# Fourier, RWKV mix and Mish MLP on one core: output steps in thirds, weight sums made earlier, another layout for the last tile

## The chip, the cores and the metric

The kernel runs on one core of a Trainium2 chip, as one program with one launch. The metric is the time of one execution on the device in microseconds (us). The engines of the core run side by side and wait for each other by semaphores: TensorE (PE, with its weight loads shown as PEld), VectorE (DVE), ScalarE (ACT), GpSimd (POOL) and SyncE (SP), which issues most of the DMAs.

## The reference

Three layers run one after another over 4 sequences of 3072 tokens with 256 channels:

```
X = rfft(x, axis=1);  Y = shrink(X mixed by w_r, w_i, plus biases);  a = irfft(Y)
xk, xr = mixes of a[token] and a[token - 1]
m = sigmoid(xr @ w_r) * (relu(xk @ w_k)**2 @ w_v)              # RWKV channel mix, 256 -> 1024 -> 256
h = m @ w_in;  out = (h * tanh(softplus(h))) @ w_out             # Mish MLP, 256 -> 2048 -> 256
```

The kernel writes each operand of a large product as a high and a low part and adds three products (high by high, low by high, high by low).

## The kernel before, in words

The program has three stages. The Fourier stage (to about 276 us) and the mix (to about 936 us) prepare the input `x2d` of the MLP in DRAM. The MLP (from there to the end) takes 24 tiles of 512 tokens.

**The mix** loops over 32 tiles `t` of 384 tokens, each in four sub-steps `i2` = 0 to 3. In a sub-step TensorE computes two blocks of `kp` (`emit_k`), and then two blocks of `vp` from the squared `kp` of two sub-steps before (`emit_v`). In sub-step 1 it also computes the gate `pp` (`emit_r`). ScalarE turns `kp` into `kr` (relu), `kh` and `kr` again (squares), and VectorE makes `kl`, the low part. In sub-step 2 VectorE multiplies the finished `vp` of the tile before by its gate into `r` (`v_ev`). The `vp` of the next tile goes to the same PSUM bank, so its first weight load waits for that `r`. The MLP's weights are decoded and split into parts in the gaps of this loop: a queue `bgq` of generators is advanced by `bg(n)`, n steps in each sub-step, 4, 1, 2 and 3 of them. A step is one instruction or two on VectorE or ScalarE, or none (some only let a load come in). Each engine runs its instructions in the order in which the program emits them.

**The MLP** works on pairs of 128 hidden rows, the steps `P` = 8t + q (q = 0 to 7 within a tile). In tile 0 the first product is made in the plain way (`emit_h`). From tile 1 on it is made by Strassen and Winograd's scheme (`emit_hS`): seven products of half-blocks instead of eight, for which sums of input blocks (`make_xS`) and of weight blocks (`WS`, and one that overwrites a part of `WI`) are needed. The second product (`o_steps`) of step P - 3 is dealt out among the first product of step P: `o(n1)`, `o(n2)` and `o(99)` take as many matmuls from it at three places. Even steps from 8 on use Strassen's scheme there too (`strassen`), with 21 matmuls of 256 columns. The others take 12 matmuls of 512 columns. A step P that is odd therefore carries the 21 small matmuls of the even step P - 3, and an even step the 12 large ones. I call them odd and even steps.

The three places cover three reads of a PSUM bank `xy` that TensorE writes again afterwards:

```
prod(xy[:, 0, :], A(0, 0), 0, start=True);  copy z <- xy on ScalarE;     o(n1)
prod S_(1), S_(2), A(0, 1);                 copy ub <- xy on ScalarE;    o(n2)
prod S_(0);                                 z <- xy + ub on VectorE;     o(99)
prod S3, A(1, 1)
```

So the first weight load of `S_(1)` waits for the copy `z`, that of `S_(0)` for the copy `ub`, and that of `S3` for the addition `z`. n1 and n2 were 3 and 2 products (9 and 6 matmuls, 6 left) in odd steps, and 5 and 3 matmuls (4 left) in even ones.

The weight sums `WS` are made by `make_WS` on VectorE and ScalarE, for a quarter of the hidden rows each: three quarters in steps 2, 4 and 6 of tile 0, and the last quarter over steps 8 to 11. Results of a tile leave by `put_out`: two transposes on VectorE and 16 DMAs of 32 KB in pieces of 256 bytes. For the last tile that comes after the last matmul, with the DMAs dealt out to three queues.

Of the kernel before, what the change touches and what calls it, by code (L numbers as in the profile page):

```python
# [29 lines left out]
def kernel(  # L30
# [887 lines left out]
    for t in range(NA + 1):  # L918
# [5 lines left out]
        for i2 in range(4):  # L924
# [47 lines left out]
            bg((4, 1, 2, 3)[i2])  # L972
# [29 lines left out]
    def make_WS(q, late=False):  # L1002

        if late:
            both = w2p.tile([128, 2, 1024], F32, tag="x2h", name="was", bufs=1)
            a, sm = both[:, 0].rearrange("p (j r i n) -> p j r i n", j=2, r=2, i=2), both[:, 1]
            sm = sm.rearrange("p (r k n) -> p r k n", r=2, k=4)
        else:
            a = pb.tile([128, 2, 2, 2, 128], F32, tag="S", name="wa", bufs=1)
            sm = pb.tile([128, 2, 4, 128], F32, tag="HS", name="ws", bufs=1)  # L1010
        w = WI[:, :, :, 512 * q:512 * (q + 1)]
        fl = a.rearrange("p j r i n -> p j (r i n)")
        nc.vector.tensor_tensor(out=fl, in0=w[:, :, 0, :], in1=w[:, :, 1, :], op=ALU.add)
        yield
        for k, x0, x1, op in (
            (0, a[:, 0, :, 1, :], a[:, 1, :, 1, :], ALU.add), (1, sm[:, :, 0, :], a[:, 0, :, 0, :], ALU.subtract),
            (2, a[:, 0, :, 0, :], a[:, 0, :, 1, :], ALU.subtract), (3, a[:, 1, :, 0, :], sm[:, :, 1, :], ALU.subtract),
        ):
            nc.vector.tensor_tensor(out=sm[:, :, k, :], in0=x0, in1=x1, op=op)
        yield  # L1020
        hi, lo = (
            (
                (WS[:, 2 * q:2 * q + 2, :, l, :], sm[:, :, 0:3, :]),
                (w[:, 0, l, :].rearrange("p (r i n) -> p r i n", r=2, i=2)[:, :, 1, :], sm[:, :, 3, :]),
            ) for l in range(2)
        )
        for h, v in hi:
            nc.scalar.copy(out=h, in_=v)
        yield
        for (h, _), (l, v) in zip(hi, lo):  # L1030
            nc.vector.tensor_tensor(out=l, in0=v, in1=h, op=ALU.subtract)

    xS_t, xT_t = {}, {}

    def make_xS(t, k, eng=None):

        v = x2_t[t]
        b11, b12, b21, b22 = (v[:, j, 256 * h:256 * h + 256] for j in range(2) for h in range(2))
# [4 lines left out]
        raw = [  # L1043
            [(xS[:, l, 0, :], b11), (xS[:, l, 1:3, :], v[:, 1, :].rearrange("p (h n) -> p h n", h=2))]
            for l in range(2)
        ]

        def sub(o, x0, x1):
            nc.vector.tensor_tensor(out=xT[:, o, :], in0=x0, in1=x1, op=ALU.subtract)

        def cast(o, x):
            if eng is None:
                nc.vector.tensor_copy(out=o, in_=x)
            else:
                eng.copy(out=o, in_=x)

        if k == 0:
            sub(0, b12, b11)
            sub(2, b22, b12)
        elif k == 1:  # L1060
            sub(1, b22, xT[:, 0, :])
            sub(3, b21, xT[:, 1, :])
        elif k == 2:
            cast(xS[:, 0, 3:7, :], xT)
        elif k == 3:
            nc.vector.tensor_tensor(out=xS[:, 1, 3:7, :], in0=xT, in1=xS[:, 0, 3:7, :], op=ALU.subtract)
        elif k == 4:
            for xs, b in raw[0]:
                cast(xs, b)
        else:  # L1070
            for (xl, b), (xh, _) in zip(raw[1], raw[0]):
                nc.vector.tensor_tensor(out=xl, in0=b, in1=xh, op=ALU.subtract)
# [9 lines left out]
    def strassen(P):  # L1082
        return P >= 8 and P % 2 == 0
# [80 lines left out]
    def put_out(t, engs):  # L1164
# [6 lines left out]
        n = 0  # L1171
        for m in range(4):
# [3 lines left out]
            for i in range(4):  # L1176
                engs[n % len(engs)].dma_start(
# [3 lines left out]
                n += 1  # L1181

    def act_1(P):
        t, r = divmod(P, 8)
        if r == 2 and t > 1:
            new_U(t - 1)
            nc.scalar.copy(out=U_t[t - 1][:, 0, :], in_=o_t[t - 1][2][:, 0, :])
        mish_xy(P - 1)

    def dve_1(P):  # L1190
        t, r = divmod(P, 8)
        if r == 2 and t > 1:
            first_sums(t - 1)
        if r == 3 and t > 0:
# [10 lines left out]
        if r == 7 and t > 0:  # L1205
            put_out(t - 1, (nc.sync,))
# [13 lines left out]
    def emit_hS(P, o):  # L1220
# [16 lines left out]
        n1, n2 = (3, 2) if strassen(P - LAG) else (5, 3)  # L1237
# [23 lines left out]

    def o_steps(P):
# [27 lines left out]
        for k in (1, 6, 5, 7, 2, 4, 3) if q == 0 else (1, 2, 4, 6, 5, 7, 3):  # L1290
# [5 lines left out]
            yield  # L1296
# [37 lines left out]
    last_sums(NBLK - 1)  # L1334
    put_out(NBLK - 1, (nc.sync, nc.scalar, nc.gpsimd))
# [82 lines left out]
```

## Time and profile before

| what | value |
|---|---|
| median of 3 runs | 1947.49 us (1946.81 to 1949.35) |
| the profiled execution | 1950.29 us, of which the span shown by the profile is 1948.5 us |
| TensorE busy, weight loads busy | 1924.0 us (99%), 1812.8 us (93%) |
| VectorE, ScalarE, GpSimd busy | 1360.7 us (70%), 1291.6 us (66%), 134.2 us (7%) |
| chain that ended last | TensorE 97%, DMA 1%, ScalarE 1%, VectorE 1% |

A busy TensorE here is an engine with a matmul in its pipeline. Matmuls overlap, so the share does not tell how closely they follow each other. That is read from the start times of consecutive matmuls and weight loads. The granted clock of TensorE (PEclk) is a share of full speed, 1.00 for 2.4 GHz and 0.50 for 1.2 GHz.

### The profile page before, as it was taken

What the parts mean: (1) busy time and instruction counts of PE and PEld (TensorE: products, weight loads), DVE (VectorE), ACT (ScalarE), POOL (GpSimd) and SP (SyncE); (2) the same over time, 40 slices, a digit from 0 to 9 for tenths busy, and PEclk for the clock granted to TensorE, in tenths of its full rate; (3) what the DMA queues carried; (4) which work ended last, traced back from release to release, by engine and by line L of the source; (5) the groups of instructions that cost most, each with busy time, mean ns of one, the idle gap of its engine ahead of it and who ended that gap; (6) DMA issues with size and microseconds to landing.
All of it is one profiled execution on the core that took longest, in us unless ns stands there. A gap on an engine that the chain in (4) does not pass through costs nothing.

```text
span 1948.5 us, 32822 instructions
## 1 busy us (share of the span) xinstructions
PE 1924.0 (99%) x12718; PEld 1812.8 (93%) x12718; DVE 1360.7 (70%) x2384; ACT 1291.6 (66%) x2244; POOL 134.2 (7%) x241
## 2 busy tenths in 40 slices
PE   7999999999999999999999999999999999999998
PEld 5888889999999999999799999999999999999997
DVE  2788775655656656644587877777777778777776
ACT  3666666666666666666467777667777667777664
POOL 0444430000000000000000000000000000000000
PEclk8999999999999999999999999999999999999999
DMA  9777532112222221211100011110011110010101
GB/s 285 218 238 229 164 101 72 60 61 61 69 61 63 80 73 56 65 50 36 63 22 23 23 28 28 30 26 23 22 31 26 30 26 23 23 32 24 30 15 22
DMA packets 114912, 127.23 MB, mean 65 GB/s; under 512 B 60722, under 2 KB 90644, under 8 KB 114756
## 3 DMA queue, kind: packets, MB, share of 16 engines
q1 hardware_dynamic: 110292, 112.22, 20.2%
q0 software_dynamic: 3744, 12.75, 1.8%
q8 instruction: 100, 1.64, 0.4%
q14 instruction: 56, 0.46, 0.1%
q10 hardware_dynamic: 720, 0.16, 0.0%
HBM read 72.65 MB, written 52.43 MB: 64 GB/s over the span
## 4 chain that ended last, share of the span: by engine, by line
PE 97%; DMA 1%; ACT 1%; DVE 1%; SPq 0%; issue 0%; POOL 0%; DVEq 0%; POOLq 0%
PE o L1272 26%; PE xy L1231 21%; PE kp L718 14%; PE vp L903 14%; PE mxp L440 4%; PE pp L857 3%; PE z L1231 3%; PE pp L541 3%; PE s2p L384 2%; PE i1p L482 2%; PE s1p L335 2%; PE k1p L440 2%; DMA XS<-in_x_dram 1%; PE hp L823 1%; DMA yc<-in_w_i_dram 0%; PE h0p L823 0%
## 5 line engine op out<-in xcount | busy, mean ns | idle before, releaser
L1272 PE MATMUL o<-gh,WO 128*128 128x512 f32 (+1 forms) x1168 | 321.3, 359 | 0.0
L718 PE MATMUL kp<-xk,WK 128*128 128x384 f32 x1524 | 291.9, 339 | 0.0
L890 DVE TENSOR_TENSOR kl<-kr,kh 128x768 fp32r<-128x768 f32 x128 | 123.0, 961 | 232.1 <-ACT kr L889 232.1
L903 PE MATMUL vp<-kh,WV 128*128 128x384 f32 x1024 | 280.4, 335 | 0.0
L718 PEld LDWEIGHTS kp<-xk,WK 128*128 128x128 f32 x1524 | 264.1, 188 | 0.6 <-ACT yT L550 0.4
L1231 PE MATMUL xy<-xS,WS 128*128 128x256 f32 x1656 | 257.6, 282 | 3.6 <-ACT z L1239 3.5
L1231 PEld LDWEIGHTS xy<-xS,WS 128*128 128x128 f32 x1656 | 235.9, 190 | 20.8 <-ACT z L1239 4.2
L1231 PE MATMUL xy<-xS,WI 128*128 128x256 f32 x1656 | 237.2, 287 | 0.0
L1096 DVE TENSOR_TENSOR gl<-g,gh 128x512 fp32r<-128x512 f32 x368 | 222.7, 615 | 20.5 <-ACT g L1094 20.4
L1231 PEld LDWEIGHTS xy<-xS,WI 128*128 128x128 f32 x1656 | 212.8, 188 | 20.1 <-DVE z L1115 5.1
L1272 PEld LDWEIGHTS o<-gh,WO 128*128 128x128 f32 x1168 | 200.8, 189 | 18.4
L1272 PE MATMUL o<-gl,WO 128*128 128x512 f32 (+1 forms) x584 | 209.3, 358 | 0.0
L1094 ACT ACTIVATE gh<-z 128x512 fp32r<-128x512 f32 x184 | 110.3, 599 | 144.4 <-DVE z L1115 87.9
L903 PEld LDWEIGHTS vp<-kh,WV 128*128 128x128 f32 x1024 | 186.7, 188 | 0.2 <-DVE r L911 0.2
L1115 DVE TENSOR_TENSOR z<-xy,ub 128x256 f32<-128x256 f32 x184 | 79.4, 432 | 135.8 <-PE xy L1231 125.5
L903 PE MATMUL vp<-kl,WV 128*128 128x384 f32 x512 | 171.5, 335 | 0.0
L888 ACT ACTIVATE kh<-kr 128x768 fp32r<-128x768 f32 x128 | 108.2, 845 | 95.4 <-PE vp L903 95.2
L1245 ACT COPY ub<-xy 128x512 f32<-128x512 f32 x184 | 108.1, 588 | 89.3 <-PE xy L1231 89.3
L881 ACT ACTIVATE kr<-kp 128x768 f32<-128x768 f32 x127 | 103.4, 814 | 70.6 <-PE kp L718 68.5
L1272 PE MATMUL o<-HS,WT 128*128 128x256 f32 x828 | 128.5, 282 | 0.0
L1272 PEld LDWEIGHTS o<-gl,WO 128*128 128x128 f32 x584 | 110.5, 189 | 9.2
L1115 DVE TENSOR_TENSOR HS<-S,HS 128x1024 fp32r<-128x1024 f32 x92 | 111.8, 1216 | 0.3 <-ACT HS L1134 0.2
(176 smaller groups left out, 3555.1 us busy)
## 6 DMA issues: line engine op xcount, KB each, us to landing
scr<-Cs SPq DMA_DIRECT2D x48, 256.0 KB, 2.4
D<-scr SPq DMA_DIRECT2D x32, 384.0 KB, 3.8
x2d<-r POOLq DMA_DIRECT2D x32, 384.0 KB, 2.8
x<-x2d SPq DMA_DIRECT2D x24, 512.0 KB, 3.9
out_dram<-ob SPq DMA_DIRECT2D x374, 32.0 KB, 1.6
A<-scr SPq DMA_DIRECT2D x44, 256.0 KB, 3.7
xs<-in_x_dram SPq DMA_DIRECT2D x24, 384.0 KB, 5.6
scr<-xs SPq DMA_DIRECT2D x24, 384.0 KB, 3.9
```

The lines of the kernel that those rows point to most:

```text
L440: nc.tensor.matmul(out=out, lhsT=a, rhs=w, start=(start and i == 0), stop=(stop and i == len(ts) - 1))
L718: nc.tensor.matmul(out=p, lhsT=WK[:, dh, w, f * 128:(f + 1) * 128], rhs=hl[:, v, dh, :], start=(i == 0), stop=(i == 5),)
L881: nc.scalar.activation(out=kr, in_=kp_t.pop(P)[:, :, 0:TA], func=AF.Relu)
L888: nc.scalar.activation(out=kh, in_=kr, func=AF.Square)
L890: nc.vector.tensor_tensor(out=kl, in0=kr, in1=kh, op=ALU.subtract)
L903: nc.tensor.matmul(out=p[:, o, 0:TA], lhsT=WV[:, f, w, o * 128:(o + 1) * 128], rhs=v[:, m, :], start=(f == 0 and i == 0), stop=(f == 7 and ...
L1094: nc.scalar.activation(out=h[:, v[1], :], in_=src[:, v[0], :], func=AF.Mish)
L1096: lambda: nc.vector.tensor_tensor(out=gl[:, hs[1], :], in0=g[:, hs[1], :], in1=gh[:, hs[1], :], op=ALU.subtract)
L1115: nc.vector.tensor_tensor(out=out, in0=x0, in1=x1, op=op)
L1231: nc.tensor.matmul(out=out, lhsT=a(l), rhs=xS[:, v, b, :], start=(start and n == 0), stop=False, skip_group_check=True)
L1245: nc.scalar.copy(out=ub, in_=xy)
L1272: nc.tensor.matmul(out=out, lhsT=w, rhs=v, start=start, stop=False, skip_group_check=True)
```

## The change

It has three parts.

1. **Output steps.** In Strassen steps `o_steps` now yields after each matmul, and not after each product of three. The 21 matmuls of an odd step are dealt out as 7, 7 and 7, and the 12 of an even one as 4, 4 and 4.
2. **Weight sums.** `make_WS` is gone from the MLP. A new generator `bg_S` makes the same sums for an eighth of the hidden rows at a time within the mix, behind the weights that it needs, and stores them in DRAM (`ws_d`). The MLP loads them by 16 DMAs on SyncE's queue. `bg` now takes 2 steps in sub-step 1 (it was 1).
3. **Last tile.** Its second product has the tokens on the output's partitions (`last_steps`): the activations are the stationary operand and `WO`, high and low parts side by side, is the moving one, 8 times 512 and 256 columns in each step. It uses no Strassen scheme, so `strassen` is false for this tile. `make_xS` puts its tokens in another order, by reading floats that stand 32 apart. As each block of 128 tokens is finished, `last_out` adds the two halves (ScalarE copies one, VectorE adds the other) and stores them by one DMA of 128 KB.

```diff
+    def bg_S(pool, w, r):
+        w = w[:, :, :, 256 * r:256 * r + 256]
+        a = pool.tile([128, 2, 2, 128], F32, tag="dec_v", name="wa", bufs=1)
+        sm = pool.tile([128, 4, 128], F32, tag="dec_b", name="ws", bufs=1)
+        nc.vector.tensor_tensor(
+            out=a.rearrange("p j i n -> p j (i n)"), in0=w[:, :, 0, :], in1=w[:, :, 1, :], op=ALU.add
+        )
+        yield
+        for k, x0, x1, op in (
+            (0, a[:, 0, 1], a[:, 1, 1], ALU.add), (1, sm[:, 0], a[:, 0, 0], ALU.subtract),
+            (2, a[:, 0, 0], a[:, 0, 1], ALU.subtract), (3, a[:, 1, 0], sm[:, 1], ALU.subtract),
+        ):
+            nc.vector.tensor_tensor(out=sm[:, k, :], in0=x0, in1=x1, op=op)
+            if k % 2:
+                yield
+        hl = pool.tile([128, 4, 2, 128], F32R, tag="wt", name="wshl", bufs=1)
+        nc.scalar.copy(out=hl[:, :, 0, :], in_=sm)
+        yield
+        nc.vector.tensor_tensor(out=hl[:, :, 1, :], in0=sm, in1=hl[:, :, 0, :], op=ALU.subtract)
+        yield
+        nc.sync.dma_start(out=ws_d[r], in_=hl.rearrange("p k l d -> p (k l d)").bitcast(F32))
...
+        for r in (2 * q, 2 * q + 1):
+            bgq.append(bg_S(pap, WI, r))
...
-            bg((4, 1, 2, 3)[i2])
+            bg((4, 2, 2, 3)[i2])
...
-    def make_WS(q, late=False):
...
+    def load_WI(r):
+        nc.sync.dma_start(
+            out=WI[:, 0, :, 256 * r + 128:256 * r + 256].bitcast(F32),
+            in_=ws_d[r][:, 768:1024].rearrange("p (l n) -> p l n", l=2),
         )
...
+    def last_order(a, how="p (c w n) -> p c w n"):
+        return a.rearrange(how, n=4, w=32)
...
+        last = t == NBLK - 1
+        o4 = last_order if last else (lambda a, how=None: a)
+        b11, b12, b21, b22 = (
+            o4(v[:, j, 256 * h:256 * h + 256], "p (c n w) -> p c w n") for j in range(2) for h in range(2)
+        )
...
     def strassen(P):
-        return P >= 8 and P % 2 == 0
+        return 8 <= P < 8 * (NBLK - 1) and P % 2 == 0
...
-        n1, n2 = (3, 2) if strassen(P - LAG) else (5, 3)
+        n1, n2 = (7, 7) if strassen(P - LAG) else (3, 2) if P - LAG >= 8 * (NBLK - 1) else (4, 4)
...
+    def last_steps(q, o, gh, gl):
+        for m in (2, 3, 0, 1):
+            for m2 in range(2):
+                f = 2 * q + m2
+                ms = slice(m * 128, (m + 1) * 128)
+                nc.tensor.matmul(out=o[m], lhsT=gh[:, m2, ms], rhs=WO[:, f], start=(f == 0), stop=False)
+                nc.tensor.matmul(
+                    out=o[m][:, 0, :], lhsT=gl[:, m2, ms], rhs=WO[:, f, 0, :], start=False, stop=(f == 15)
+                )
+                if q == 7 and m2:
+                    last_out(m, o[m])
+                yield
...
+    def last_out(m, o):
...
+        nc.scalar.copy(out=v, in_=o[:, 1])
+        nc.vector.tensor_tensor(out=v, in0=v, in1=o[:, 0], op=ALU.add)
...
+        nc.sync.dma_start(out=out_v[b, j, k].rearrange("n w d -> w n d"), in_=ob)
...
                 mm(o[bank][:, half, :], w(l), rhs, q == 0 and bank not in begun)
                 begun.add(bank)
-            yield
+                yield
...
     load_x2(1)
+    for r in range(8):
+        nc.sync.dma_start(out=WS[:, r].bitcast(F32).rearrange("p k l d -> p (k l d)"), in_=ws_d[r][:, 0:768])
+    for r in range(2):
+        load_WI(r)
     for i in range(4):
         nc.sync.dma_start(out=WT[:, i].bitcast(F32).rearrange("p k l d -> p (k l d)"), in_=wt_d[i])
...
-                if P == 8:
-                    last_WS = make_WS(3, True)
                 emit_hS(P, o)
-                if P < 12:
-                    next(last_WS, None)
...
-                if q in (2, 4, 6):
-                    for _ in make_WS(q // 2 - 1):
-                        pass
+                load_WI(P)
...
-    last_sums(NBLK - 1)
-    put_out(NBLK - 1, (nc.sync, nc.scalar, nc.gpsimd))
```

On TensorE an odd step stood like this before, from the last three of its first nine output matmuls on (`o<-...` are output matmuls; `xy<-xS,WS x6` are `S_(1)` and `S_(2)`, `xy<-xS,WS x3` is `S_(0)`, and `xy<-xS,WI x9` begins with `S3` and ends with the next step's first product):

```order
L1272 MATMUL o_9562<-gh,WT 128x256 x2
L1272 MATMUL o_9562<-gl,WT 128x256
L1231 MATMUL xy<-xS,WS 128x256 x6
L1231 MATMUL z<-xS,WI 128x256 x3
L1272 MATMUL o_9564<-HS,WT 128x256 x3
L1272 MATMUL o_9565<-HS,WT 128x256 x3
L1231 MATMUL xy<-xS,WS 128x256 x3
L1272 MATMUL o_9565<-HS,WT 128x256 x3
L1272 MATMUL o_9563<-HS,WO 128x256 x3
L1231 MATMUL xy<-xS,WI 128x256 x9
```

The same odd step on TensorE now, from the seventh and last of its first output matmuls on:

```order
L1312 MATMUL o_9633<-gh,WT 128x256
L1241 MATMUL xy<-xS,WS 128x256 x6
L1241 MATMUL z<-xS,WI 128x256 x3
L1312 MATMUL o_9633<-gh,WT 128x256
L1312 MATMUL o_9633<-gl,WT 128x256
L1312 MATMUL o_9635<-HS,WT 128x256 x3
L1312 MATMUL o_9636<-HS,WT 128x256 x2
L1241 MATMUL xy<-xS,WS 128x256 x3
L1312 MATMUL o_9636<-HS,WT 128x256 x4
L1312 MATMUL o_9634<-HS,WO 128x256 x3
L1241 MATMUL xy<-xS,WI 128x256 x9
```

Two matmuls left the first group, and one was added to each of the other two, so seven stand ahead of `S3` where six stood.

ScalarE in sub-steps 0 and 1 of the mix's tile 7 before (`yT` is the next tile's input, `r<-pp` the gate at the start of sub-step 2):

```order
L550 COPY yT<-pp 128x3x128
L881 ACTIVATE kr<-kp 128x768
L888 ACTIVATE kh<-kr 128x768
L889 ACTIVATE kr<-kr 128x768
L550 COPY yT<-pp 128x3x128
L881 ACTIVATE kr<-kp 128x768
L888 ACTIVATE kh<-kr 128x768
L889 ACTIVATE kr<-kr 128x768
L866 ACTIVATE r<-pp 128x768
```

ScalarE at the same place now:

```order
L574 COPY yT<-pp 128x3x128
L165 CAST wshl<-ws 128x4x128
L907 ACTIVATE kr<-kp 128x768
L914 ACTIVATE kh<-kr 128x768
L915 ACTIVATE kr<-kr 128x768
L574 COPY yT<-pp 128x3x128
L165 CAST wshl<-ws 128x4x128
L907 ACTIVATE kr<-kp 128x768
L914 ACTIVATE kh<-kr 128x768
L915 ACTIVATE kr<-kr 128x768
L892 ACTIVATE r<-pp 128x768
```

In each of these two sub-steps a cast of weight sums now stands ahead of the relu `kr<-kp`. VectorE in sub-step 1 of the same tile now, from the `kl` of sub-step 0 on:

```order
L916 TENSOR_TENSOR kl<-kr,kh 128x768
L585 TENSOR_TENSOR dl<-yT 128x768
L161 TENSOR_TENSOR ws<-wa 128x128
L161 TENSOR_TENSOR ws<-wa,ws 128x128
L916 TENSOR_TENSOR kl<-kr,kh 128x768
L937 TENSOR_TENSOR r<-r,vp 128x768
```

Two subtractions of `bg_S` stand between `dl` and `kl` (one decoding instruction stood there before), and ScalarE's second cast reads what they write.

## Rows read from the trace of the kernel before

**Rows 1.** Windows: us, busy of PE, PEld, DVE, ACT, POOL, PEclk, DMA, GB/s.

```profile
276.00:930.00 654.00, 654.00 (x3932) 652.87 (x3931) 377.21 (x529) 437.74 (x628) 23.90 (x32) 1.00 0.21 62
...
967.00:971.00 4.00, 0.51 (x3) 0.11 (x1) 2.47 (x6) 3.37 (x7) 0.00 (x0) 0.98 0.30 117
971.00:974.30 3.30, 3.30 (x13) 3.02 (x14) 0.82 (x1) 0.59 (x1) 0.00 (x0) 0.51 0.00 0
...
1014.00:1900.00 886.00, 885.97 (x6373) 830.32 (x6372) 698.23 (x1398) 621.66 (x1189) 0.00 (x0) 1.00 0.11 26
```

**Rows 2.** Chain of waits in one odd and one even step: start, us, what.

```profile
1387.12 0.71 PE o L1272 x6
1387.84 1.22 PE xy L1231 x9
...
1392.33 0.93 PE o L1272 x4
1393.26 1.07 PE xy L1231 x9
```

**Rows 3.** Timeline of the next odd step, around S3: start, us, what.

```profile
1397.66 0.43 DVE L1115 TENSOR_TENSOR z<-xy,ub 128x256 f32<-128x256 f32 x1 [0.94 <-PE xy L1231]
1397.75 0.52 PE L1272 MATMUL o<-HS,WO 128*128 128x256 f32 x3
...
1398.15 0.55 PEld L1231 LDWEIGHTS xy<-xS,WI 128*128 128x128 f32 x4
```

**Rows 4.** Timeline, copy z and the load of S_(1): even step, then odd.

```profile
1389.15 0.36 ACT L1239 COPY z<-xy 128x256 f32<-128x256 f32 x1 [0.37 <-PE xy L1231]
...
1389.82 0.90 PEld L1231 LDWEIGHTS xy<-xS,WS 128*128 128x128 f32 x6
...
1394.43 0.36 ACT L1239 COPY z<-xy 128x256 f32<-128x256 f32 x1 [0.27 <-PE xy L1231]
...
1395.13 0.55 PEld L1231 LDWEIGHTS xy<-xS,WS 128*128 128x128 f32 x4
```

**Rows 5.** Waits of the weight loads, 970 to 1940 us: total, times, longest.

```profile
PEld xy L1231 <- DVE z L1115: 5.1, 23, 0.5
PEld xy L1231 <- ACT z L1239: 4.2, 2, 3.9
```

**Rows 6.** Timeline of ScalarE at step 8, start of tile 1.

```profile
967.47 0.83 ACT L1028 CAST WS<-ws 128x768 fp32r<-128x768 f32 x1 [5.16 <-DVE ws L1019]
```

**Rows 7.** Timeline of the mix, tile 10, sub-steps 1 and 2.

```profile
502.93 0.95 DVE L561 TENSOR_TENSOR dl<-yT 128x768 f32<-128x768 f32 x1
...
505.37 0.85 ACT L888 ACTIVATE kh<-kr 128x768 fp32r<-128x768 f32 x1 [1.32 <-PE vp L903]
...
507.13 0.96 DVE L890 TENSOR_TENSOR kl<-kr,kh 128x768 fp32r<-128x768 f32 x1 [3.25 <-ACT kr L889]
...
508.00 0.95 DVE L911 TENSOR_TENSOR r<-r,vp 128x768 f32<-128x768 f32 x1
...
509.11 0.19 PEld L903 LDWEIGHTS vp<-kh,WV 128*128 128x128 f32 x1
```

**Rows 8.** Groups by form: count, busy us, mean ns of one, idle before.

```profile
L881 ACT ACTIVATE kr<-kp 128x768 f32<-128x768 f32 x127 | 103.4, 814 | 70.6 <-PE kp L718 68.5
...
L141 ACT CAST wthl<-wt 128x512 fp32r<-128x512 f32 x4 | 2.5, 620 | 6.2 <-DVE wt L132 6.2
...
L132 DVE TENSOR_TENSOR wt<-dec_v,wt 128x128 f32<-128x128 f32 x8 | 2.3, 290 | 0.1
```

**Rows 9.** The end: last matmul; DMA rate, 1939.4 to 1948.5 in 40 slices.

```profile
1939.01 0.40 PE L1272 MATMUL o<-gl,WO 128*128 128x512 f32 x1
...
GB/s 0 0 0 0 0 0 0 0 0 0 0 0 109 161 107 183 134 221 231 122 228 183 177 180 168 105 0 0 0 0 0 0 0 0 0 0 0 0 0 0
```

**Rows 10.** The page's DMA issues: KB each, median us from issue to landing.

```profile
scr<-Cs SPq DMA_DIRECT2D x48, 256.0 KB, 2.4
...
out_dram<-ob SPq DMA_DIRECT2D x374, 32.0 KB, 1.6
```

More of the change, by code (lines that the diff above doesn't have):

```diff
@@ L64 @@
     wt_d = [dram.tile([128, 1024], F32, name=f"wt_{i}") for i in range(4)]
+    ws_d = [dram.tile([128, 1024], F32, name=f"ws_{r}") for r in range(8)]
     x2d = [dram.tile([128, 2, 1536], F32, name=f"x2d_{q}") for q in range(2 * B)]
@@ L1000 @@
     WT = pb.tile([128, 4, 4, 2, 128], F32R, name="WT")
-    def make_WS(q, late=False):
[L1004 to L1013, printed above, removed]
-        yield
[L1015 to L1025, printed above, removed]
-        )
[L1027 to L1031, printed above, removed]
+    def load_WI(r):
+        nc.sync.dma_start(
+            out=WI[:, 0, :, 256 * r + 128:256 * r + 256].bitcast(F32),
+            in_=ws_d[r][:, 768:1024].rearrange("p (l n) -> p l n", l=2),
+        )
     xS_t, xT_t = {}, {}
+    def last_order(a, how="p (c w n) -> p c w n"):
+        return a.rearrange(how, n=4, w=32)
     def make_xS(t, k, eng=None):
         v = x2_t[t]
-        b11, b12, b21, b22 = (v[:, j, 256 * h:256 * h + 256] for j in range(2) for h in range(2))
+        last = t == NBLK - 1
[3 more added lines that the diff above has]
+        )
         if k == 0:
@@ L1042, in make_xS, with raw, xt @@
         xT, xS = xT_t[0], xS_t[t]
[L1043 to L1046, printed above, removed]
+        def raw(l):
+            if last:
+                return [(o4(xS[:, l, i, :]), b) for i, b in enumerate((b11, b21, b22))]
+            return [(xS[:, l, 0, :], b11), (xS[:, l, 1:3, :], v[:, 1, :].rearrange("p (h n) -> p h n", h=2))]
+        def xt(o):
+            return o4(xT[:, o, :])
         def sub(o, x0, x1):
-            nc.vector.tensor_tensor(out=xT[:, o, :], in0=x0, in1=x1, op=ALU.subtract)
+            nc.vector.tensor_tensor(out=xt(o), in0=x0, in1=x1, op=ALU.subtract)
         def cast(o, x):
@@ L1060, in make_xS @@
         elif k == 1:
-            sub(1, b22, xT[:, 0, :])
-            sub(3, b21, xT[:, 1, :])
+            sub(1, b22, xt(0))
+            sub(3, b21, xt(1))
         elif k == 2:
@@ L1067, in make_xS @@
         elif k == 4:
-            for xs, b in raw[0]:
+            for xs, b in raw(0):
                 cast(xs, b)
         else:
-            for (xl, b), (xh, _) in zip(raw[1], raw[0]):
+            for (xl, b), (xh, _) in zip(raw(1), raw(0)):
                 nc.vector.tensor_tensor(out=xl, in0=b, in1=xh, op=ALU.subtract)
@@ L1117, in sums @@
     def sums(P, k):
-        if not (strassen(P) and P < 8 * NBLK):
+        if not strassen(P):
             return
@@ L1162, in last_sums, with put_out @@
                 nc.vector.tensor_copy(out=u, in_=o)
-    def put_out(t, engs):
+    def put_out(t):
         U = U_t.pop(t)
@@ L1170, in put_out @@
             )
-        n = 0
         for m in range(4):
@@ L1176, in put_out @@
             for i in range(4):
-                engs[n % len(engs)].dma_start(
+                nc.sync.dma_start(
                     out=dst[:, :, 64 * i:64 * i + 64],
@@ L1180, in put_out @@
                 )
-                n += 1
     def act_1(P):
         t, r = divmod(P, 8)
-        if r == 2 and t > 1:
+        if r == 2 and 1 < t < NBLK:
             new_U(t - 1)
@@ L1191, in dve_1 @@
         t, r = divmod(P, 8)
-        if r == 2 and t > 1:
+        if r == 2 and 1 < t < NBLK:
             first_sums(t - 1)
-        if r == 3 and t > 0:
+        if r == 3 and 0 < t < NBLK:
             if t == 1:
@@ L1204, in dve_1 @@
                 load_x2(t + 2)
-        if r == 7 and t > 0:
-            put_out(t - 1, (nc.sync,))
+        if r == 7 and 0 < t < NBLK:
+            put_out(t - 1)
         low(P - 1)
@@ L1260, in new_o @@
         o_t[t] = [psb.tile([128, 2, 256], F32, tag=f"o{m}", name=f"o{m}") for m in range(4 if t else 2)]
+    def last_steps(q, o, gh, gl):
[10 more added lines that the diff above has]
+                yield
+    last_ob = []
+    def last_out(m, o):
+        if not last_ob:
+            last_ob.append(pb.tile([128, 4, 256], F32, tag="ob", name="ob", bufs=1))
+        ob = last_ob[0][:, m, :]
+        v = ob.rearrange("p (d e) -> p e d", e=2)
+        o = o.rearrange("p l (e d) -> p l e d", e=2)
+        nc.scalar.copy(out=v, in_=o[:, 1])
+        nc.vector.tensor_tensor(out=v, in0=v, in1=o[:, 0], op=ALU.add)
+        b, r = divmod(4 * (NBLK - 1) + m, 24)
+        j, k = divmod(r, 3)
+        nc.sync.dma_start(out=out_v[b, j, k].rearrange("n w d -> w n d"), in_=ob)
     def o_steps(P):
@@ L1268, in o_steps @@
         gh, gl = g_t.pop(P)[0:2]
+        if t == NBLK - 1:
+            yield from last_steps(q, o, gh, gl)
+            return
         wv = WO[:, 2 * q:2 * q + 2].rearrange("p m l (e d) -> p m l e d", e=2)
@@ L1295, in o_steps @@
                 begun.add(bank)
-            yield
+                yield
     LAG = 3
     load_x2(1)
+    for r in range(8):
+        nc.sync.dma_start(out=WS[:, r].bitcast(F32).rearrange("p k l d -> p (k l d)"), in_=ws_d[r][:, 0:768])
+    for r in range(2):
+        load_WI(r)
     for i in range(4):
```

## The prediction

> **What bounds the kernel now.** I read the windows by stage first. TensorE is busy all the time in the mix and in the tiles of the MLP, while VectorE and ScalarE are busy for 58 and 67% of the mix and 79 and 70% of the tiles [rows 1]. So only two things count: what TensorE is given to do, and the places where it waits. Work on another engine counts only where TensorE waits for it. The reader should look for such places in three views.
>
> The chain of waits shows the first. In an odd step the nine matmuls from `S3` on take 1.22 us, in an even step 1.07 [rows 2]. Each odd step loses 0.15 us there. The timeline says to what: the addition `z` ends at 1397.66 + 0.43 = 1398.09, and the load for `S3` begins at 1398.15, 0.05 us behind it. The last output matmul ahead of it began at about 1397.99, and the load would have followed that at once [rows 3]. The list of waits leaves this out, since it is shorter than the gaps it counts.
>
> The second place is in the list: weight loads waited for the copy `z` twice, 4.2 us in all and 3.9 at once [rows 5]. That is step 8. ScalarE stood for 5.16 us in front of the cast of `make_WS`, which waited for VectorE's sums, and the copy was queued behind it [rows 6]. TensorE was busy for 0.51 of 4.00 us, and in the next 3.30 us its granted clock was 0.51, the 1.2 GHz level [rows 1]. The third place is the end: the last matmul begins at 1939.01, and the last bytes leave 26 slices of 0.2275 us after 1939.4, at 1945.3 [rows 9].
>
> **The change part by part.** A small matmul costs 1.07 / 9 = 0.119 us of TensorE's time, a large one 0.93 / 4 = 0.2325 [rows 2].
>
> *Thirds in odd steps.* Seven matmuls instead of six stand ahead of `S3`. The addition `z` keeps its distance from `S_(0)`, as VectorE stood idle for 0.94 us before it [rows 3]. So the wait falls from 0.15 to about 0.04 us, by one matmul, 0.119. The first third gets two fewer, which moves the load of `S_(1)` from 1395.13 to 1394.89. The copy `z` ends at 1394.79, and with the 0.05 us of the handover at `S3` the load is free from 1394.84. That leaves 0.05 us [rows 3, 4]. The cover of the copy is nearly gone, then; what it costs if it goes is the second rival. `S_(0)` gets one matmul more behind the copy `ub`. The steps concerned are P = 11, 13, ..., 185, that is 88: 88 x 0.119 = 10.5 us gained (0 if the copy comes 0.12 us later, 13 if the whole wait went).
>
> *Thirds in even steps.* 4, 4, 4 leaves the cover of `S3` as it was. The load of `S_(1)` moves up by 0.23 to 1389.59; it is free from 1389.15 + 0.36 + 0.05 = 1389.56 [rows 4], and it would have another 0.11 us, since it runs beside a large matmul. I count 0.
>
> *Weight sums out of the MLP.* The cast that ScalarE waited for is gone, and I expect both waits to go. Of the 4.00 us TensorE gets 3.5 back, 0.3 for the second wait (4.2 - 3.9), and half of the 3.30 us at half clock, 1.6 [rows 1, 5]: 5.4 us. What is late next there is the copy itself behind the activations of step 7, which can run during the 12 large output matmuls (2.8 us) between them. The new loads of `WS` are queued on SyncE at the start of the MLP, 30 us ahead of step 8; the slowest nearby price is 2.4 us for 256 KB [rows 10], and eight of 384 KB one after another would be some 29 us at that rate, of which step 8 needs only the first. I count nothing for them. The first loads of `WI` stand behind them on that queue and wait for TensorE's reads, and the load of x for tile 2 stands behind those of steps 2 to 5, which are past by then.
>
> *Weight sums in the mix.* There are 40 new steps, eight sets of an addition, four subtractions, a cast and a subtraction. VectorE has 277 us idle in the mix [rows 1], so their length costs nothing by itself; their place does. The thin chain is in sub-steps 1 and 2: `kh` waits for TensorE, and then `kr`, `kl` and `r` follow without a gap. `r` ends at 508.95, and the load of `vp` begins at 509.11 [rows 7]. Less a handover of 0.05, 0.11 us are left. VectorE has 3.25 us idle before that `kl`, so a second VectorE instruction in sub-step 1 is free. A cast on ScalarE is not, if it waits for subtractions of the same sub-step: they follow `dl`, which ends at 503.88, end at 503.88 + 2 x 0.29 = 504.46, the cast at 504.46 + 0.05 + 0.62 = 505.13, the relu behind it 0.81 later at 505.94 [rows 7, 8], and `kh` begins near 505.95 instead of 505.37. TensorE then waits about 0.58 - 0.11 = 0.47 us, or 0.3 if instructions of VectorE and ScalarE overlap a little. Counting the 296 steps out in elevens, such a pair falls in sub-step 1 twice: at tile 7 (`bg_S`, the casts in the order of ScalarE above) and at tile 25 (`bg_T`). That is 0.8 us lost. In the other sub-steps the queue had such pairs before, and the loads waited for nothing that `r` or a cast explains. From below 0, from above 27 tiles with a second step at 0.6 us each (the fourth rival).
>
> *Last tile.* Its eight output steps took 4 x 21 x 0.119 + 4 x 12 x 0.2325 = 21.2 us. They become 64 pairs of a large and a small matmul, 64 x 0.3515 = 22.5: 1.3 lost. In steps 187, 189 and 191 three pairs (1.05 us) now stand ahead of `S3` where 0.71 stood, so 0.15 goes three times: 0.9 us lost in all. At the end, transposes and 16 DMAs on three queues give way to a copy (0.36) [rows 4], an addition (0.43) [rows 3] and one DMA of 128 KB behind the last matmul (0.40). Small and larger stores take 1.6 us for 32 KB and 2.4 for 256 KB [rows 10]; I take 2.0, between them. With two handovers that is 3.3 us from the last matmul's start to the last byte, where 6.3 stood: 3.0 gained (2.6 to 3.4). The 3.2 us after the last byte stay.
>
> Reads of floats 32 apart are not in the trace. Floats two apart take 0.29 us for 128 [rows 8], on the line of 0.43 for 256 in a row [rows 3]. The Trainium skill, "SBUF — State Buffer", in its note on cachelines, says that a line holds 16 bytes and each access that crosses to a new line pays. No run here shows that, as two apart share a line.
>
> **Sum.** -10.5 - 5.4 + 0.8 + 0.9 - 3.0 = -17.2. The profiled execution took 1950.29 us (span 1948.5), so it would take 1933.1. The median of the runs, 1947.49, is 2.8 below the profiled one, and gives **1930.3 us**.
>
> **Rivals.**
> 1. *The forecast*: 1930.3, own range 1927.5 to 1933. Chance 0.64.
> 2. *The copy `z` takes the place of the addition `z`* in odd steps. Against it are 0.05 us of margin, for it that this is all there is. If the load of `S_(1)` is freed 0.17 us later than I have it, all 10.5 are given back: 1940.8; half of it, 1935.5. Chance 0.12.
> 3. *Step 8 waits all the same*, now for loaded sums or for ScalarE: 5.4 back, 1935.7. Against it: ScalarE had no other work there. Chance 0.08.
> 4. *The mix becomes slower*: the second step of sub-step 1 delays `kh`, `kl` or `r` in all of the 27 tiles with steps, not in two. It decides from (17.2 + 0.8) / 27 = 0.67 us a tile, about one VectorE or ScalarE step without the margin of 0.11: 27 x 0.7 would give 1948.4, and 0.8 each 1951. The 3.25 us idle before `kl` speak against it. Chance 0.04.
> 5. *More gain*, as when the whole 0.15 goes and the 0.8 of the mix do not come: 1927. Chance 0.07.
> 6. *Reads 32 apart are dear.* Two subtractions in an odd step of tile 22 stand ahead of an addition `z` with 0.94 us to spare [rows 3]: at twice the time (+0.84) nothing is lost, at four times (+2.5) 1.6 us, and some 6 in the four steps that hold such work: 1936. This is what that page's note would do here. Chance 0.05.
>
> Chances: a difference under 0.2% (3.9 us) can't be told from none. Faster (below 1943.6) are all but the fourth and the tail of the second: 0.94; the same 0.02; slower 0.04. The range 1926.5 to 1936.5 holds the first, third, fifth and sixth cases and half of the second, nearly 0.9.
>
> **What would show it.** In the profile after, the nine matmuls from `S3` on should take about 1.11 us in odd steps, and a tile of eight steps 4 x 0.119 less than before. The wait of 3.9 us at step 8 and the stretch at half clock behind it should be gone. In the mix, short waits of `vp` loads for `r` should stand in tiles 7 and 25 alone. From the last matmul's start to the last byte should be 3.3 us. I am wrong if loads of `S_(1)` wait for `z`, if step 8 waits for a DMA, or if the mix becomes longer by more than 2 us.

## The result, and the profile after

| | median | executions |
|---|---|---|
| before | 1948.42 us | 4, 1946.81 to 1949.67 |
| after | 1931.93 us | 4, 1929.77 to 1933.43 |

The ratio is 0.9915, with a 95% interval of 0.9898 to 0.9932: 16.5 us faster, where 17.2 were forecast, and 1931.93 us where 1930.3 stood. The profiled execution of after took 1929.77 us (span 1928.0), that of before 1950.29.

Spans of single executions can't be set against each other to a microsecond, though. The Fourier stage, from the first matmul to the first `kp` matmul, took 274.96 us in the profile of before and 271.61 in that of after. Over the thirteen profiles of this study it took 270.7 to 275.5, although no kernel changes that stage. So I compare the profiles by stretches between matmuls (and the copies `z`) that both kernels have:

```
stretch                                        before     after   after - before   forecast
Fourier stage                                  274.96    271.61       -3.35           -
mix, first kp to last vp matmul                659.33    660.27       +0.94         +0.8
last vp matmul to first matmul of step 8        30.22     30.22        0.00           -
first matmul of step 8 to copy z of step 16     48.03     43.27       -4.76  } -14.6  -15.8
copy z of step 16 to that of step 184          876.30    866.50       -9.79  }
copy z of step 184 to the last matmul           48.97     49.79       +0.82         +0.8
last matmul's start to the end                   9.51      5.14       -4.37         -3.0
sum without the Fourier stage                                        -17.16        -17.2
```

The two in brackets hold step 8 (forecast 5.4) and 87 of the 88 odd steps (10.4 of 10.5). 84 of them lie in the second one and gave 9.79, or 0.117 each. So the three in the first gave 0.35, and 4.4 are left for step 8. One odd step lies in the stretch of the last tile, which lost 0.94 without it. Measured from copy `z` to copy `z` over those 84 pairs, odd steps fell from 5.148 to 5.020 us, by 0.128, and even ones rose from 5.284 to 5.295, by 0.011.

The windows of after answer to [rows 1] (columns as there; the second window holds the whole wait of step 8, whose first matmul starts at 963.30, and the third follows it):

```profile
276.00:930.00 654.00, 653.96 (x3927) 651.71 (x3926) 394.24 (x577) 440.34 (x634) 23.89 (x32) 1.00 0.22 68
962.67:966.67 4.00, 3.09 (x19) 2.44 (x18) 1.23 (x1) 2.34 (x5) 0.00 (x0) 1.00 0.62 176
966.67:970.00 3.33, 3.33 (x23) 2.95 (x21) 0.47 (x2) 1.56 (x3) 0.00 (x0) 1.00 0.09 25
1008.00:1889.00 881.00, 880.89 (x6403) 831.22 (x6402) 702.54 (x1403) 624.31 (x1196) 0.00 (x0) 1.00 0.11 26
```

The stretch behind step 8 now runs at a granted clock of 1.00, where it was 0.51 (1.2 GHz). TensorE is busy for 3.09 of 4.00 us, where it was busy for 0.51. A part of the wait is still there. The chain of waits through an odd and an even step (start, us, what) answers to [rows 2]:

```profile
1386.40 0.84 PE o L1312 x7
1387.23 1.10 PE xy L1241 x9
...
1391.61 0.93 PE o L1312 x4
1392.54 1.09 PE xy L1241 x9
```

The nine matmuls from `S3` on take 1.10 us in the odd step instead of 1.22. The forecast was 1.11. The timeline of the next odd step answers to [rows 3, 4]:

```profile
1393.72 0.36 ACT L1249 COPY z<-xy 128x256 f32<-128x256 f32 x1 [0.28 <-PE xy L1241]
...
1394.18 0.79 PEld L1241 LDWEIGHTS xy<-xS,WS 128*128 128x128 f32 x6
...
1396.83 0.43 DVE L1127 TENSOR_TENSOR z<-xy,ub 128x256 f32<-128x256 f32 x1 [0.28 <-PE xy L1241]
...
1397.31 1.13 PEld L1241 LDWEIGHTS xy<-xS,WI 128*128 128x128 f32 x9
```

The copy `z` ends at 1394.08, and the load of `S_(1)` follows at 1394.18 without a wait. It is 0.10 us behind, as forecast, and 0.05 of that is the handover. `S3` still begins 0.05 us behind the end of the addition (1396.83 + 0.43 = 1397.26), so it still waits a little, 0.037 us by the median of the odd steps.

The waits of the weight loads answer to [rows 5] (total, times, longest):

```profile
PEld xy L1241 <- DVE z L1127: 4.6, 23, 0.3
PEld xy L1241 <- ACT z L1249: 1.4, 1, 1.4
```

The copy `z` is still waited for once, at step 8, and the timeline there shows why:

```profile
963.08 0.39 PE L1312 MATMUL o<-gl,WO 128*128 128x512 f32 x1
...
963.28 0.60 ACT L871 ACTIVATE gh<-hp 128x512 fp32r<-128x512 f32 x1 [3.37 <-PE o L1312]
...
964.36 0.40 PE L1312 MATMUL o<-gh,WO 128*128 128x512 f32 x1
964.73 0.61 ACT L872 ACTIVATE g<-hp 128x512 f32<-128x512 f32 x1
965.20 0.42 ACT L1249 COPY z<-xy 128x256 f32<-128x256 f32 x1
...
965.67 0.76 PEld L1241 LDWEIGHTS xy<-xS,WS 128*128 128x128 f32 x6 [1.35 <-ACT z L1249]
```

ScalarE was idle for 3.37 us before the first activation of step 7, and what ended that was an output matmul, the last of step 7. The last matmul of the first product that the activations read had ended at 960.74. So four activations stand in front of the copy `z`, and TensorE loses 1.08 us.

In the mix, four tiles became longer: by 0.15 (tile 7), 0.32 (tile 11), 0.16 (tile 16) and 0.27 us (tile 23). The loads of `vp` that waited for `r` were one before and three after, in tiles 7, 11 and 23 (total, times, longest):

```profile
PEld vp L903 <- DVE r L911: 0.2, 1, 0.2
...
PEld vp L929 <- DVE r L937: 0.7, 3, 0.3
```

Tile 7 looks as forecast:

```profile
417.35 0.95 DVE L585 TENSOR_TENSOR dl<-yT 128x768 f32<-128x768 f32 x1
...
418.22 0.29 DVE L161 TENSOR_TENSOR ws<-wa 128x128 f32<-128x128 f32 x1
418.42 0.29 DVE L161 TENSOR_TENSOR ws<-wa,ws 128x128 f32<-128x128 f32 x1
418.74 0.62 ACT L165 CAST wshl<-ws 128x512 fp32r<-128x512 f32 x1 [1.94 <-DVE ws L161]
419.26 0.80 ACT L907 ACTIVATE kr<-kp 128x768 f32<-128x768 f32 x1
420.10 0.85 ACT L914 ACTIVATE kh<-kr 128x768 fp32r<-128x768 f32 x1
...
423.74 0.19 PEld L929 LDWEIGHTS vp<-kh,WV 128*128 128x128 f32 x1 [0.20 <-DVE r L937]
```

The cast waits for the subtractions, and the relu and `kh` stand behind it. TensorE waited 0.20 us for it, not 0.47. From the end of `dl` (418.30) to `kh` it took 1.80 us where 2.07 were added up, because each instruction here starts up to 0.1 us before the one ahead of it on its engine has ended: the second subtraction at 418.42 (the first ends at 418.51), the relu at 419.26 (the cast ends at 419.36). Tile 11 was not foreseen. There an addition, four subtractions and their cast all fall in sub-step 0, and its relu begins so late that sub-step 1 is late as well:

```profile
496.67 0.68 DVE L153 TENSOR_TENSOR wa<-WI 128x512 f32<-128x512 f32 x1
...
498.44 0.62 ACT L165 CAST wshl<-ws 128x512 fp32r<-128x512 f32 x1 [1.97 <-DVE ws L161]
498.97 0.81 ACT L907 ACTIVATE kr<-kp 128x768 f32<-128x768 f32 x1
```

Tile 16 was not foreseen either. There the four subtractions of `bg_T` and their cast now fall together in sub-step 3. ScalarE is late from there on, and in the next sub-step TensorE waits for its copy `yT`:

```profile
616.78 0.62 ACT L142 CAST wthl<-wt 128x512 fp32r<-128x512 f32 x1 [3.02 <-DVE wt L133]
...
621.22 0.97 PEld L565 LDWEIGHTS pp<-ift,D 96*128 96x128 f32 x8 [0.36 <-ACT yT L574]
```

Before, this same tile had the one wait for `r` of 0.2 us shown above, which is gone.

The end of the kernel answers to [rows 9], by the last operations of the timeline and the DMA rate from 1922 to 1928 us in 40 slices of 0.15:

```profile
1922.86 0.28 PE L1278 MATMUL o<-WO,gl 128*128 128x256 f32 x1
...
1923.18 0.38 ACT L1293 COPY ob<-o 128x256 f32<-128x256 f32 x1 [0.32 <-PE o L1278]
1923.60 0.42 DVE L1294 TENSOR_TENSOR ob<-ob,o 128x256 f32<-128x256 f32 x1 [0.28 <-ACT ob L1293]
```

```profile
GB/s 0 0 0 0 0 0 0 0 0 0 102 335 341 96 0 273 341 246 14 157 362 301 55 61 355 341 116 0 0 0 0 0 0 0 0 0 55 0 0 0
```

The last bytes of the results leave 27 slices after 1922, at 1926.05 (the 55 behind them are one packet of another queue). That is 3.2 us after the last matmul's start, where 3.3 were forecast. But the program ends 1.95 us after them, not 3.2 us as before.

### The profile page after: what moved, and what is told of

Read it like the earlier page. It is cut to its first block, busy times and chain, and to the rows that moved or that the text cites. A ratio compares the mean times of both kernels' runs of the same rounds, so it can differ in the third digit from the quotient of the medians.

```text
span 1928.0 us, 32868 instructions
## 1 busy us (share of the span) xinstructions
PE 1911.6 (99%) x12714; PEld 1807.1 (94%) x12714; DVE 1352.5 (70%) x2382; ACT 1289.7 (67%) x2244; POOL 131.7 (7%) x236
## 4 chain that ended last, share of the span: by engine, by line
PE 97%; DMA 1%; ACT 1%; DVE 0%; SPq 0%; issue 0%; DVEq 0%; ACTq 0%
PE o L1312 25%; PE xy L1241 21%; PE kp L742 14%; PE vp L929 14%; PE mxp L464 4%; PE pp L883 3%; PE z L1241 3%; PE pp L565 3%; PE s2p L408 2%; PE i1p L506 2%; PE s1p L359 2%; PE k1p L464 2%; DMA XS<-in_x_dram 1%; PE hp L849 1%; PE o L1277 1%; PE o L1278 0%
## 5 line engine op out<-in xcount | busy, mean ns | idle before, releaser
L1241 PE MATMUL xy<-xS,WI 128*128 128x256 f32 x1656 | 229.7, 283 | 0.1
L1312 PEld LDWEIGHTS o<-gh,WO 128*128 128x128 f32 x1120 | 192.1, 188 | 17.8
L1312 PE MATMUL o<-gl,WO 128*128 128x512 f32 (+1 forms) x560 | 200.9, 359 | 0.0
L1312 PE MATMUL o<-HS,WT 128*128 128x256 f32 x792 | 123.1, 282 | 0.0
L1312 PEld LDWEIGHTS o<-gl,WO 128*128 128x128 f32 x560 | 105.6, 189 | 9.0
L1106 ACT ACTIVATE g<-xy 128x512 f32<-128x512 f32 x184 | 111.6, 606 | 0.0
```

Source lines behind the costliest of these rows:

```text
L1106: nc.scalar.activation(out=h[:, v[1], :], in_=src[:, v[0], :], func=AF.Mish)
L1241: nc.tensor.matmul(out=out, lhsT=a(l), rhs=xS[:, v, b, :], start=(start and n == 0), stop=False, skip_group_check=True)
L1312: nc.tensor.matmul(out=out, lhsT=w, rhs=v, start=start, stop=False, skip_group_check=True)
```

## Experiments

Each is the kernel after with one edit, so they are set against after (ratio to before 0.9915). Within the MLP, two profiles of the very same kernel differed by 0.7 us. The kernels under step 8, the end and the mix were executed once each, so they are read by stretches of their profiles and not by their times.

**Each part undone.** The output steps (the length of a step is the mean time from its copy `z` to the next):

```diff
-        n1, n2 = (7, 7) if strassen(P - LAG) else ... (4, 4)
+        n1, n2 = (3, 2) if strassen(P - LAG) else ... (5, 3)
...
-                yield
+            yield
```

> The kernel after with part 1 undone (thirds as before: 3 and 2 products of three in odd steps, 5 and 3 matmuls in even ones). Theory (the thirds give back one small matmul's time ahead of S3 in each of 88 odd steps, 0.117 us each in the trace after): 10.3 us longer than the kernel after, about 1942.2 us; odd steps 0.13 us longer than after, the even ones 0.01 to 0.02 shorter, since loads there wait a little more now. Rival (the even steps or the finer interleaving bring a part of it): odd steps less than 0.10 longer and even steps longer too.

1940.71 us, ratio 0.9963 (0.9948 to 0.9977). From step 8 to the last matmul it took 9.1 us longer. Odd steps took 5.139 us instead of 5.020 (+0.119), even ones 5.282 instead of 5.295 (-0.013). Both signs are the theory's, and the size is 1.2 us short of it, 0.01 in each odd step. The rival needed longer even steps, and falls. The chain shows the old odd step again, 1.21 us from `S3` on:

```profile
1392.02 0.71 PE o L1312 x6
1392.74 1.21 PE xy L1241 x9
```

The weight sums (`make_WS` back in the MLP, `bg_S` and its loads out):

```diff
-        for r in (2 * q, 2 * q + 1):
-            bgq.append(bg_S(pap, WI, r))
...
-            bg((4, 2, 2, 3)[i2])
+            bg((4, 1, 2, 3)[i2])
...
+                if P == 8:
+                    last_WS = make_WS(3, True)
```

> The kernel after with part 2 undone (weight sums made in the MLP by make_WS, none in the mix, sub-step 1 with one step). Theory: the stretch from step 8's first matmul to the copy z of step 16 gets back the 3.65 us wait and the half clock, 4.4 us longer than after; the mix 0.94 us shorter: 3.5 us longer in all, about 1935.4. Rival (the wait at step 8 was one of the particular order of before, not of make_WS): the stretch changes by less than 1.5 us, and the time is within 1 us of the kernel after.

1935.35 us, 0.9934 (0.9919 to 0.9949). The stretch from step 8 to step 16 took 5.2 us longer and the mix 0.94 us shorter (659.33, as in before to 0.01). So the rival falls. The 5.2 us are 0.8 more than the theory's 4.4; the list of waits has two more of them than before (4 instead of 2, 5.2 us instead of 4.2), and what makes these two is open. The weight loads waited for the copy `z` again, and the cast stood before the activations:

```profile
PEld xy L1264 <- ACT z L1272: 5.2, 4, 4.2
```

```profile
964.04 0.83 ACT L1052 CAST WS<-ws 128x768 fp32r<-128x768 f32 x1 [5.16 <-DVE ws L1043]
```

The last tile (Strassen steps, transposes and 16 stores on three queues again):

```diff
-        last = t == NBLK - 1
+        last = False
...
+    last_sums(NBLK - 1)
+    put_out(NBLK - 1, (nc.sync, nc.scalar, nc.gpsimd))
```

> The kernel after with part 3 undone (last tile with Strassen steps, transposes and 16 DMAs on three queues). Theory: from the last matmul's start to the end 9.5 us instead of 5.1, the steps of the last tile 0.8 us shorter: 3.6 us longer in all, about 1935.5. Rival (the floats 32 apart cost something in tile 22 that is given back here): tile 22 is more than 0.2 us shorter than in the kernel after.

1933.95 us, 0.9929 (0.9914 to 0.9943). From the last matmul to the end it took 9.84 us (+4.7), and the last tile 1.3 us less: 3.4 us longer for the two. The last tile gave back 0.5 us more than expected because its odd steps have the thirds here: four times 0.117 us less than the 48.97 us of before make 48.50, and 48.52 were measured. So against a Strassen tile with thirds the new layout costs 1.3 us. Tile 22, where the floats 32 apart are read, took 41.23 us against 41.27 (41.16 in the second profile of after), so no cost of theirs can be seen there.

**Where the limits of the odd step lie.** One matmul more ahead of `S3`, and two fewer ahead of `S_(1)`:

```diff
-        n1, n2 = (7, 7) if strassen(P - LAG) else ...
+        n1, n2 = (7, 6) if strassen(P - LAG) else ...
```

> The kernel after with 7, 6, 8 matmuls in odd steps instead of 7, 7, 7. Theory (S3 still waits 0.037 us for the addition z, S_(0) has 0.28 us from the copy ub, of which 0.05 are needed): an eighth matmul ahead of S3 takes the last 0.037 us away, odd steps 0.037 us shorter, 88 x 0.037 = 3.3 us less, about 1928.6. Rival (the 0.037 us is a fixed cost of the change from output matmuls to S3, no wait): odd steps within 0.01 us of the kernel after, total the same.

1926.79 us, 0.9893 (0.9876 to 0.9909). Odd steps took 4.984 us instead of 5.020, 0.037 less as expected, and the load for `S3` no longer waits. From step 8 to the last matmul it is 4.1 us less, where 3.3 were expected; even steps, whose matmuls are dealt out as in after, were 0.009 us shorter too (5.286). The chain has 1.06 us from `S3` on, about the 1.07 of an even step before:

```profile
1384.27 0.95 PE o L1312 x8
1385.22 1.06 PE xy L1241 x9
```

```diff
-        n1, n2 = (7, 7) if strassen(P - LAG) else ...
+        n1, n2 = (5, 8) if strassen(P - LAG) else ...
```

> The kernel after with 5, 8, 8 matmuls in odd steps instead of 7, 7, 7. Theory (the load of S_(1) begins 0.10 us behind the end of the copy z and needs 0.05, so only 0.05 us of its cover are left): two matmuls fewer ahead of it, 0.24 us, make it wait 0.19 us, and S3 saves its 0.04: odd steps 0.15 us longer, 88 x 0.15 = 13 us more than the kernel after, about 1945. Rival (the load of S_(1) is not held by the copy z): odd steps no longer than in the kernel after, total 0 to 3.5 us less.

1942.24 us, 0.9962 (0.9947 to 0.9976). The load of `S_(1)` now begins 0.051 us behind the end of the copy `z`, 0.187 us late. In the chain, the group that took 0.71 us takes 0.89:

```profile
1398.65 0.59 PE o L1312 x5
1399.24 0.89 PE xy L1241 x6
```

Odd steps took 0.136 longer and even ones 0.015 shorter: 10.6 us more from step 8 to the last matmul, not 13. The mechanism is as expected: the copy's cover was down to 0.05 us.

**Even steps.**

```diff
-        ... (4, 4)
+        ... (4, 3)
```

> The kernel after with 4, 3, 5 matmuls in even steps instead of 4, 4, 4. Theory (S3 waits 0.055 us for the addition z in three even steps of a tile and 0.16 in the one whose addition is queued behind sums of outputs; S_(0) has 0.28 us from the copy ub and needs 0.05, a large matmul is 0.2325): both S3 waits go, S_(0) has just enough: a tile 0.3 us shorter, 6.5 us less than the kernel after, about 1925.5. Rival (the 0.055 us is a cost of the change of matmuls and no wait): only the one step a tile becomes shorter, 0.16 us, 3.5 us less.

1929.81 us, 0.9903 (0.9889 to 0.9918). Within the MLP it is 0.6 us less, no more than two profiles of one kernel differ. My theory failed, and so did the rival. The intervals between the loads tell why. In three of the four even steps of a tile of the kernel after, the load for `S3` comes 0.286 us behind the one before it, 0.054 late, and the next one 0.173 behind that; the two make 0.459, hardly less than two large matmuls (0.465). With 4, 3, 5 the wait for the addition is gone there and the intervals are 0.233 and 0.232, in sum the same. So a load that is 0.05 us late behind a large matmul delays no matmul. Behind a small one it does, as the kernel with 7, 6, 8 showed. In the fourth of these steps (q = 2) the wait stays: the load comes 0.380 us behind the one before it, where it came 0.383. VectorE works without a gap there, so the addition follows the instructions ahead of it and comes no earlier when `S_(0)` is done earlier:

```profile
1348.23 1.28 DVE L1108 TENSOR_TENSOR gl<-g,gh 128x512 fp32r<-128x512 f32 x2
1349.43 0.43 DVE L1127 TENSOR_TENSOR z<-xy,ub 128x256 f32<-128x256 f32 x1
...
1349.91 0.53 PEld L1241 LDWEIGHTS xy<-xS,WI 128*128 128x128 f32 x4 [0.19 <-DVE z L1127]
```

**Step 8.**

```diff
+                if q == 7:
+                    o(99)
                 emit_h(P)
```

> The kernel after with the output matmuls of step 7 ahead of its first product instead of behind it. Theory (at step 8 the copy z is queued behind the four activations of step 7, and these wait for the output matmuls that read the buffer of gh they write): the activations start while the first product still runs, and of the 1.08 us that TensorE waits at step 8 about 0.4 stay: 0.7 us less from step 8 to step 16. Rival (the activations wait for the end of the first product or for a load): the wait at step 8 stays at 1.0 us or more.

From step 8 to step 16 it took 0.73 us less, and TensorE waited 0.32 us at step 8 instead of 1.08. The first activation now starts while the first product runs:

```profile
962.25 2.88 PE L849 MATMUL hp<-x2h,WI 128*128 128x512 f32 x12
...
963.81 0.60 ACT L871 ACTIVATE gh<-hp 128x512 fp32r<-128x512 f32 x1 [2.24 <-PE hp L849]
...
966.59 0.78 PEld L1241 LDWEIGHTS xy<-xS,WS 128*128 128x128 f32 x6 [0.60 <-ACT z L1249]
```

**The end.**

```diff
-        nc.sync.dma_start(out=out_v[b, j, k].rearrange("n w d -> w n d"), in_=ob)
+        (nc.gpsimd if m == 1 else nc.sync).dma_start(out=out_v[b, j, k].rearrange("n w d -> w n d"), in_=ob)
```

> The kernel after with the very last store (block m = 1) on GpSimd's queue instead of SyncE's. Theory (of the 1.3 us that the end gained without having been forecast, most is that GpSimd no longer issues DMAs there: its drain ended 3.35 us behind its last issue in the kernel before): last matmul to end 0.9 us longer than after, 6.0 instead of 5.1. Rival (the end is shorter because fewer stores have to be waited for): the end within 0.3 us of the kernel after.

From the last matmul to the end it took 5.71 us instead of 5.14. That lies between theory and rival, and in kernels with the end of after this stretch took 4.83 to 5.61, so the time alone decides nothing. The records of the drains, by which the engines close the program, do (count, shortest, median and longest in ns, first and last start):

```profile
L1449 POOLq DRAIN  x3: 40/102/3497, 1928.1 to 1932.1; - x3
L1449 SPq DRAIN  x3: 7/7/7, 1930.5 to 1931.8; - x3
```

SyncE was through 3.9 us after the last matmul (4.4 in after, where it had the last store as well), and GpSimd's long drain ended 1.0 us later, 2.9 us behind its issue. In the kernel before, too, it ended 1.0 us later than SyncE, and in the kernel with the last tile undone, which has stores on GpSimd's queue as well, 0.5 us later; in after it adds nothing. So GpSimd holds up the end by 0.5 to 1.0 us. Here 0.5 of that was made up, since its store did not queue behind one of SyncE's. Why its drain takes so long is not shown.

**The mix.**

```diff
-            bg((4, 2, 2, 3)[i2])
+            bg((4, 1, 3, 3)[i2])
```

> The kernel after with 4, 1, 3, 3 steps of background work in the sub-steps of the mix instead of 4, 2, 2, 3 (what falls in sub-steps 0 and 3 stays the same). Theory (the mix lost 0.15 us at tile 7 and 0.27 at tile 23 to subtractions and their cast together in sub-step 1, and 0.35 at tile 11 to an addition, four subtractions and a cast together in sub-step 0): the waits of tiles 7 and 23 go, that of tile 11 stays, the mix 0.4 us shorter, 659.85 instead of 660.27. Rival (any step added to sub-steps 1 and 2 costs): the mix stays or is longer, with new waits at other tiles.

The mix took 659.79 us, 0.48 less. Tiles 7 and 23 are back at 20.56, tile 11 stays at 20.83 (20.88 in after) and tile 16 at 20.85: the theory, tile by tile.

**Together**, with 7, 6, 8, the edits of step 8 and the mix, and the last store on ScalarE's queue:

> The kernel after with 7, 6, 8 in odd steps, the output matmuls of step 7 ahead of its first product, background steps 4, 1, 3, 3, and the very last store on ScalarE's queue. If the parts add up: 4.1 (as measured) + 0.73 (as measured) + 0.4 + 0.3 (the last store's issue no longer waits 0.3 us for the one before it on SyncE) = 5.5 us less than the kernel after. If they get in each other's way (ScalarE's issue late behind its copies, other waits in the mix): 4.5 or less.

> The kernel after once more, unchanged, for comparison on the same chip: ratio to the kernel before 0.9915 again, within 0.001; from step 8 on and in the mix the same to 0.1 us, the Fourier stage anywhere in 271 to 276 us.

On one chip this kernel took 1925.43 us (1924.59 to 1927.27; ratio to before 0.9888, 0.9871 to 0.9904), and the kernel after 1931.44 (1929.70 to 1934.17; 0.9917, 0.9902 to 0.9931). It is 6.0 us faster, and no execution of the one reaches those of the other. By the stretches without the Fourier stage it is 5.4 us; the three parts measured alone make 5.3 (4.1, 0.73 and 0.48). The last store on ScalarE's queue shows no gain that can be told apart: last matmul to end 5.04 us. The second profile of after did not repeat the mix to 0.1 us: 661.01, with 0.69 us lost once, in tile 0.

## Why the prediction was right, and where it was not

- *Thirds in odd steps*: right in place and nearly in size, 10.3 us by the stretches (10.5 forecast) and 9.1 by undoing the part. The 10.3 are net: an odd step gained 0.128 us, and an even one lost 0.011. The 0.05 us of margin of the copy `z` was real: 7, 7, 7 lies just inside it, 5, 8, 8 beyond it.
- *Thirds in even steps*: nothing, as counted. The load of `S_(1)` begins 0.09 us behind the copy's end there, so it does not wait, and the reason given, that a load beside a large matmul has time to spare, was not needed; it was shown for `S3` (the kernel with 4, 3, 5). The 0.011 us that even steps lost do not come from their thirds alone: with 5, 8, 8 they have 4, 4, 4 as well and took 5.280 us.
- *Weight sums out of the MLP*: 4.4 us instead of 5.4. The step that failed is "the copy itself behind the activations of step 7, which can run during the 12 large output matmuls". I had looked at what stands ahead of the copy on ScalarE, but not at what these activations wait for. `gh` of step 7 takes the buffer of step 4 (two buffers in turn for steps with P % 3 < 2), and the output matmuls that read it are the last thing in step 7. So the activations start behind them. The third rival, a step 8 that waits all the same, came true by a fifth.
- *Weight sums in the mix*: +0.94 for +0.8, in size by luck. The mechanism was right, and a cast behind subtractions of its own sub-step is what costs. But tile 7 cost 0.15, not 0.4, and the second pair fell in tile 23, not 25 (my count of the steps ran off behind tile 14): 0.42 for the two, where 0.8 stood. The rest, 0.48, comes from two events that were not in the sum at all, in sub-step 0 of tile 11 and sub-step 3 of tile 16. That "the loads waited for nothing that `r` or a cast explains" was a misreading, too: before, one load had waited 0.2 us for `r`, in tile 16.
- *Last tile*: +0.94 for +0.9. Of the gain set against it, the 0.15 us in three steps, most would have come from the thirds alone: undoing this part gave 1.3 us back.
- *The end*: -4.4 for -3.0. To the last byte the terms hold. "The 3.2 us after the last byte stay" failed: 1.95 stay. By the records of the drains, 1.0 of the difference is GpSimd, which no longer has stores at the end, and 0.2 is SyncE, which is through 1.2 us behind the last bytes where it took 1.4.
- *Reads 32 apart* are dearer, 1.5 to 1.7 times. That is below the twofold at which the sixth rival still loses nothing, and no effect on the time was seen.

The two misses, 1.2 us too much in the MLP (1.0 of them at step 8) and 1.4 too little at the end, cancel. That the sum came out within 0.1 us is chance; the terms were good to about 1.4 us.

## What to carry over

When a wait is taken away, ask of the instruction that is late next what *it* waits for, buffers included; its place in its queue is not enough. In a loop that one engine bounds, write down the margin of each handover: it tells how many matmuls may move and where to stop (here one more was to be had, and two fewer cost 10.6 us). And for the last stores of a program, look at what the engine of their queue still does behind them: here GpSimd ended 0.5 to 1.0 us after SyncE, while between SyncE's queue and ScalarE's no difference could be told.

## What was not expected of the hardware

- Reads of floats 32 apart, 128 x 256: 0.63 to 0.69 us instead of 0.42 on VectorE, as this group of lines shows (min, median, max in ns; the maximum is the last tile's), and 0.67 to 0.69 instead of 0.41 on ScalarE.

```profile
L1061 DVE TENSOR_TENSOR xT<-x x6: 418/420/693, 1755.2 to 1838.2; 128x256 f32<-128x256 f32 x6
```

  That is 1.5 to 1.7 times. The Trainium skill, "Advanced Engine Details and Errata", section "Memory Cachelines", says that accesses which each meet another 16-byte line pay a penalty. The trace agrees, and gives its size.
- GpSimd's drain ended 3.3 us (before), 3.7 us (last tile undone) and 2.9 us (its store last) behind the last DMA that it issued, and 1.0, 0.5 and 1.0 us behind SyncE's.
- A weight load 0.04 us late cost 0.04 us behind a matmul of 256 columns, and one 0.05 late nothing behind one of 512.
- Undoing the odd steps' gain gave 0.013 us back in each even step, and in the kernels with 7, 6, 8 and 5, 8, 8 even steps were 0.009 and 0.015 shorter than in after. What does that was not found; the second profile of after itself is 0.004 shorter.
